# Tails' product before the seven products, weight parts issued a step later, normalisation queued a step behind its transposes

## The chip, the core and the metric

The kernel runs on one core of a Trainium2 chip. The metric is the time of one execution on the device, in microseconds (us). The engines are named as in the profile: PE (TensorE matmuls) with PEld (its weight loads), DVE (VectorE), ACT (ScalarE), POOL (GpSimd) and SP (SyncE, which issues nearly all DMAs here). Each engine takes its own instructions strictly in the order of the program; engines wait for one another at semaphores only.

## The reference

Batch 8, 8 heads, 576 tokens, head width 64, everything in float32. First an attention that keeps the 32 largest scores of every row, then a Fourier mix with a two-layer network:

```python
scores = scale * q @ k.T                       # per batch and head, 576 x 576
kth = 32nd largest score of the row
attn = softmax(where(scores >= kth, scores, -1e9))
x = (attn @ v) with the 8 heads side by side   # 8 x 576 x 512
u = x + real(fft(fft(x, axis=tokens), axis=channels))
un = (u - mean(u)) / sqrt(var(u) + 1e-6)       # per token, over 512 channels
out = u + relu(un @ w_ch1) @ w_ch2             # 512 -> 2048 -> 512
```

## The kernel before, in words

**Items and steps.** Attention goes by pairs of heads, four pairs to a batch, 32 in all. A pair has nine items: two for each of four blocks of 128 query rows (one per head), and between them one item for the two heads' 64 "tail" rows together. The list has 288 items, and the main loop takes one item per step, software-pipelined over several steps. In step i DVE finds the 32 largest scores of item i and begins those of item i+1 (L425, L427); PE makes the scores of item i+3; ACT and POOL mask item i-1 (L448, L451) and ACT exponentiates it (L459). What one step issues on an engine stands on that engine in the order in which the loop body calls it.

**Turning the weights.** For pairs 4 to 6 and 8 to 30 (`pair_by_dma`, L438) the attention weights are transposed by DMA. Two steps after its item, `plane` has ACT split the words in two halves (L472) and SP write them to DRAM (`planes<-wk`, L485 and L488); a step later `turn` has SP issue the transposing DMA (`PT<-planes`, L506). Four steps after the last item of a chunk, PE multiplies the transposed weights with v (`attend`, L564, 20 matmuls). A pair has two chunks: the first holds token blocks 0, 1 and the tails (320 columns), the second blocks 2 and 3 (256 columns).

**Back to tokens.** ACT copies the product out (L578), and `to_tokens` (L594), called two steps after `attend` (one step for the fourth pair's second chunk), has PE transpose it into the tile `tpx` (L604). That tile lies in a PSUM pool `ps_o` of one buffer, tag "o", which the product `o` of the next `attend` uses too. `normalise` (L607) then divides on DVE and writes the batch's tokens `x` (L608, L615). It is put on one of two lists: `late_now` is issued on DVE at the end of the same step, behind that step's top-32 work; `late_next` becomes `late_now` at the end of the step (L1628), so that it is issued one step later. From batch 2 on, a call of `to_tokens` is held back until batch b-2 has been stored (the `written` set); calls that were held back then follow one another in successive steps, save that steps with an `attend` take none. In batch 1 ACT normalises instead.

**The Fourier mix and the statistics.** After a batch's last item, PE multiplies with tables (`dft_tokens` L755, `dft_channels` L812 and L816), POOL adds the result to x (`add_mixed`, L836), DVE takes mean and variance (`stats`, L841), and `rsqrt` (L847) makes 1/sqrt(var) in three DVE instructions and 16 small ones on POOL. A table of plans (`at(step, where, fn)`) sets in which step each runs.

**The network as units.** `mlp_units` (L952) lists a batch's network as units, small pieces of PE work with a cost in us, which `some` hands out between the attention's PE work of the following steps so that every step gets about the same amount (`level`, L1465). A batch has two chunks of tokens, (0, 1, tails) and (2, 3). For each chunk 16 "hidden" units make the first layer (L966) into `hT`. The second layer is done in one of two ways. `back` (L986) multiplies a block of 128 tokens in eight units (L993), and the 64 tails in four (L1032), half of `hT` in each half of PSUM. `fast` (L1068) does blocks 0 and 1 together with seven products instead of eight, in 14 units `p2, p1, p5, p4, p6, p3, p7` (two parts each, L1163); it is used for the first chunk of batches 1 to 6 and for both chunks of batch 7. It needs sums of the halves of `hT` (`mix`, POOL, L1108) and sums of quarters of `w2`, which an earlier stage left in DRAM (`w_parts`). `bring` (L906) loads such a part, 512 KB per call, on SP's queue into the quarter `w2_12` or `w2_21`; it waits until PE no longer reads what lies there. `begin` (L1229) brings T1 into `w2_12`; p2 then has T4 brought into `w2_21`, p5 T2 into `w2_12`, p4 T3 into `w2_21`, and p6 and p7 bring the plain quarters (B12, B21) back. In batch 7 T4 and T3 go to a place of their own.

**The order before.** For a chunk with seven products the units are: one hidden unit, `begin`, 15 hidden units, the first `mix` (no PE work), the 14 product units, the tails' four units, and then the next chunk. The tails read all of `w2`, so in the plain form.

Two lists serve POOL: `some_sums` (L931) issues the sums within a budget per step, and `need` (L938) issues at once what a unit is about to read.

Of the kernel before, what the change touches and what calls it, by code (L numbers as in the profile page):

```python
# [73 lines left out]
def kernel(  # L74
# [9 lines left out]
    nc = tc.nc  # L84
# [509 lines left out]
    def to_tokens(pair, ch, at_once=True):  # L594

        b, hp = divmod(pair, NPB)
        if b not in x_of:
            x_of[b] = batp.tile([P, 5, DM], F32, name=f"x_{b}", tag="x", bufs=2)
        x = x_of[b]
        xT, rd = xT_of.pop((pair, ch)), rd_of.pop((pair, ch))  # L600
        shape, name = [P, 4, P], f"tpx_{pair}_{ch}"
        tp = ps_o.tile(shape, F32, name=name, tag="o") if at_once else bank(shape, name)
        for n, t in enumerate(CHUNKS[ch]):
            nc.tensor.transpose(tp[0:ROWS[t], n, :], xT[:, P * n:P * n + ROWS[t]], ident)  # L604
        cols = slice(P * hp, P * (hp + 1))

        def normalise():  # L607
            nc.vector.tensor_tensor(  # L608
                out=x[:, 2 * ch:2 * ch + 2, cols].rearrange("p t (e d) -> p t e d", e=2),
                in0=tp[:, 0:2, :].rearrange("p t (e d) -> p t e d", e=2),  # L610
                in1=rd[:, 0:4].rearrange("p (t e) -> p t e", e=2).to_broadcast([P, 2, 2, D]),
                op=ALU.mult,
            )
            if ch == 0:
                nc.vector.tensor_tensor(  # L615
                    out=x[0:TAIL, 4, cols].rearrange("p (e d) -> p e d", e=2),
                    in0=tp[0:TAIL, 2, :].rearrange("p (e d) -> p e d", e=2),
                    in1=rd[0:TAIL, 4:6].to_broadcast([TAIL, 2, D]),
                    op=ALU.mult,
                )  # L620

        def normalise_on_act():
            for n, t in enumerate(CHUNKS[ch]):
                r = slice(0, ROWS[t])
                for e in range(2):
                    hd = slice(D * e, D * (e + 1))
                    nc.scalar.mul(
                        out=x[r, t, cols][:, hd], in_=tp[r, n, hd],
                        mul=rd[r, 2 * n + e:2 * n + e + 1],
                    )  # L630


        if b == 1 and (hp, ch) != (NPB - 1, 1):
            at(now[0] + 1, "act", normalise_on_act)
        else:
            (late_now if at_once else late_next).append(normalise)
        return 0.14 * len(CHUNKS[ch])


# [207 lines left out]
    def rsqrt(b):  # L847

        vr = small.tile([P, 5], F32, name=f"vr_{b}", tag="vr", bufs=2)
        gi = small.tile([P, 5], I32, name=f"gi_{b}", tag="gi", bufs=2)  # L850
        t2 = small.tile([P, 5], F32, name=f"t2_{b}", tag="t2", bufs=2)
        rs_of[b] = rs = gi.bitcast(F32)
        nc.vector.tensor_scalar(
            out=vr, in0=mv[b % 2][:, :, 1], scalar1=1e-6, scalar2=None, op0=ALU.add
        )
        nc.vector.tensor_scalar(
            out=gi, in0=vr.bitcast(I32), scalar1=1, scalar2=None, op0=ALU.arith_shift_right
        )
        nc.vector.tensor_scalar(
            out=gi, in0=gi, scalar1=-1, scalar2=0x5F3759DF, op0=ALU.mult, op1=ALU.add  # L860
        )
        for _ in range(4):
            nc.gpsimd.tensor_tensor(out=t2, in0=rs, in1=rs, op=ALU.mult)
            nc.gpsimd.tensor_tensor(out=t2, in0=t2, in1=vr, op=ALU.mult)
            nc.gpsimd.tensor_scalar(
                out=t2, in0=t2, scalar1=-0.5, scalar2=1.5, op0=ALU.mult, op1=ALU.add
            )
            nc.gpsimd.tensor_tensor(out=rs, in0=rs, in1=t2, op=ALU.mult)

    def channels_first(b, t):  # L870

# [31 lines left out]
    scr = dramp.tile([P, len(OPS), NK, DH], F32, name="w2_parts", tag="w2_parts")  # L903
    w2_12, w2_21 = w2[:, 0:NK, DH:DM], w2[:, NK:NIT, 0:DH]

    def bring(o, place, part):  # L906
        kcs = slice(NK // 2 * part, NK // 2 * (part + 1))
        dst = place[part] if isinstance(place, list) else place[:, kcs]
        nc.sync.dma_start(out=dst, in_=scr[:, o, kcs, :])

    parts = {}

# [39 lines left out]
    def mlp_units(b):  # L952
# [16 lines left out]
                )  # L969
            nc.scalar.activation(out=hT_of[ch][:, it, :], in_=hp[:, 0:w], func=AF.Relu)  # L970

        cps, cts, stored = {}, [], []

        def ct_of(t):

# [10 lines left out]
        def back(ch, t, part):  # L986
            n, hT, rs = CHUNKS[ch].index(t), hT_of[ch], rs_of[b]
            if part == 0:
                cps[t] = bank([P, DM], f"cp_{b}_{t}", True)
            cp, free = cps[t]  # L990
            if t != 4:
                for it in range(2 * part, 2 * part + 2):
                    nc.tensor.matmul(  # L993
                        cp, lhsT=hT[:, it, P * n:P * (n + 1)], rhs=w2[:, it, :],
                        start=(it == 0), stop=(it == NIT - 1),
                    )
                if part == 7:
                    xt = x[:, t, :]

                    def store():  # L1000
                        tok = HS * (t // 2) + P * (t % 2)
                        nc.sync.dma_start(out=out[b, tok:tok + P, :], in_=xt)
                        stored.append(t)
                        if len(stored) == 4:
                            written.add(b)

                    def finish():
                        nc.vector.scalar_tensor_tensor(
                            out=xt, in0=cp, scalar=rs[:, t:t + 1], in1=xt, op0=ALU.mult, op1=ALU.add
                        )  # L1010
                        free()

                    if last:
                        finish()
                    elif t == 3:

                        late_next.append(finish)
                    else:
                        ct = ct_of(t)
                        nc.scalar.mul(out=ct, in_=cp, mul=rs[:, t:t + 1])  # L1020
                        free()
                        nc.gpsimd.tensor_tensor(out=xt, in0=xt, in1=ct, op=ALU.add)

                    if last:
                        store()
                    else:
                        at(now[0] + 2, "load2", store)
                return

            for it in range(2 * part, 2 * part + 2):  # L1030
                for g in range(2):
                    nc.tensor.matmul(  # L1032
                        cp[TAIL * g:TAIL * (g + 1), :],
                        lhsT=hT[:, NIT // 2 * g + it, P * n:P * n + TAIL],
                        rhs=w2[:, NIT // 2 * g + it, :],
                        start=(it == 0), stop=(it == NIT // 2 - 1),
                    )
            if part == 3:
                tails_done(cp, free)

        def tails_done(cp, free):

            if b and not last:
                need((b, 0, "x", 4))
            ct, rs = ct_of(4), rs_of[b]
            for h in range(2):
                r0 = TAIL + TH * h
# [20 lines left out]
        def fast(ch):  # L1068
# [123 lines left out]
            def p5(part):  # L1192
                need((b, ch, "21", part))
                c = product("v", hi, "21", first, part, False)
                bring(T2, w2_12, part)
                if part:
                    to_x(tb, hi, c, 2)

# [30 lines left out]
            def begin():  # L1229
# [2 lines left out]
                    if last:  # L1232
                        bring(T4, second, part)

            return (0.0, begin, "hidden"), [
                (0.0, lambda: mix("21", "21", "22", ALU.add), "back")
            ] + [
                (1.75, lambda f=f, part=part: f(part), "back")
# [4 lines left out]
        for ch in range(2):  # L1243
# [4 lines left out]
            seven = b and ch == 0 or last  # L1248
            if seven:
                begin, products = fast(ch)  # L1250
                units.insert(1 - NIT, begin)
                units += products
            for t in [t for t in CHUNKS[ch] if t == 4 or not seven]:
                units += [
                    (1.75, lambda ch=ch, t=t, p=p: back(ch, t, p), "back")
                    for p in range(4 if t == 4 else 8)
                ]
        return units


# [117 lines left out]
    for b in range(B):  # L1378
# [47 lines left out]
        for n, t in enumerate((0, 1, 4, 2, 3)):  # L1426
# [2 lines left out]
            at(s, "pe2", lambda b=b, t=t, q=quick: dft_channels(b, t, q), 1.75)  # L1429
            if not quick:  # L1430
                at(s, "pool2", lambda b=b, t=t: add_mixed(b, t))
                at(s + 1, "dve", lambda b=b, t=t: stats(b, t))
            at(s + (1 if quick else 2), "pe", lambda b=b, t=t: channels_first(b, t), 0.6)
            if first and t == 4:
                at(s + 1, "pe", lambda: (queue.extend(waiting), waiting.clear()) and 0.0)
        at(s + 1, "begin" if quick else "dve", lambda b=b: rsqrt(b))
        arrivals.append(s + (1 if quick else 2))
        at(arrivals[-1], "units", lambda b=b: (queue if b else waiting).extend(mlp_units(b)))

    queue, waiting, pending, written, now, out_next = [], [], [], set(), [0], []  # L1440
    step_us = 6.0

    def chunk_at(i):
# [29 lines left out]
    def run(i, where):  # L1473
        for fn in plan.pop((i, where), []):
            fn()
# [16 lines left out]
    while i < N + 5 or plan or queue or sums:  # L1492
# [71 lines left out]
            mask(i - 1)  # L1564
        plane(i - 2, 0)
        plane(i - 2, 1)
        run(i, "convert")
        if short:
            expo(i - 1)
# [98 lines left out]
```

## Time and profile before

| | us |
|---|---|
| runs (median of 3) | 1869.55 (1868.05 to 1875.36) |
| the profiled execution's own time | 1868.68 |
| its span, first to last instruction | 1866.9 |

| engine | busy us | share of the span |
|---|---|---|
| PE | 1704.1 | 91% |
| PEld | 1086.8 | 58% |
| DVE | 1584.9 | 85% |
| ACT | 1294.6 | 69% |
| POOL | 912.8 | 49% |

The mean granted TensorE clock is 0.955 of full speed. The costliest groups are DVE's top-32 rounds (L425 and L427), PE's first layer (L966, 528.3 us), POOL's masking (L451, 408.1 us) and PE's plain second layer (L993, 236.0 us). Attention ends at about 1650 us; behind that PE alone is busy, with the last batch's mix and network.

To read the views: the page gives busy times by engine, the busy share of 40 slices of the span, and the groups of instructions with the idle time just before them and what ended it. The windows give busy times in chosen stretches, the timeline the instructions of one engine in order of time (start, length, engine, line; in square brackets the idle time before it and what ended it). Rows "SPq" are SP's issues of DMAs; their length includes a wait at their head when several are merged.

### The profile page before, as it was taken

The page shows a single profiled execution, that of the slowest core. Times are in us where ns is not written, and L with a number is a line of the kernel's source. Part 1 is how long each engine was busy: PE and PEld are TensorE (multiplying, and loading weights), DVE is VectorE, ACT ScalarE, POOL GpSimd, SP SyncE. Part 2 cuts the span into 40 slices and gives each one's busy share as a digit, 9 for nine tenths or more (in the row PEclk, how much of TensorE's full clock was granted, in tenths as well). Part 3 has the DMA queues.
Part 4 walks back from the last instruction along what each step waited for, and adds up shares of the span by engine and source line. Part 5 has one row for each costly group of instructions (what it writes and reads, how often), then busy time and mean ns, then how long its engine had stood idle before and what let it go on. Part 6 is the DMA issues. An engine that isn't in the chain of part 4 may idle for free.

```text
span 1866.9 us, 26900 instructions
## 1 busy us (share of the span) xinstructions
PE 1704.1 (91%) x8134; PEld 1086.8 (58%) x8134; DVE 1584.9 (85%) x3301; ACT 1294.6 (69%) x3104; POOL 912.8 (49%) x1278
## 2 busy tenths in 40 slices
PE   5576699889899999899999999999999999999999
PEld 3344365365456555566556565666567555677677
DVE  7999989889899999999999899999999899762110
ACT  6878659577787778777787688767787678652100
POOL 4768644454745366354644465355545464341012
PEclk7777799899899999999999999999999999999999
DMA  5334016661567755586476755785467655530132
GB/s 168 104 92 115 20 45 162 168 176 26 129 157 202 188 128 130 147 208 160 118 169 169 188 127 139 154 230 133 128 162 189 161 121 146 133 106 6 51 112 72
DMA packets 516576, 249.16 MB, mean 133 GB/s; under 512 B 398288, under 2 KB 506448, under 8 KB 516432
## 3 DMA queue, kind: packets, MB, share of 16 engines
q1 hardware_dynamic: 515664, 247.23, 51.2%
q8 instruction: 65, 1.06, 0.2%
q14 instruction: 79, 0.65, 0.1%
q10 hardware_dynamic: 768, 0.21, 0.1%
HBM read 93.63 MB, written 84.74 MB: 96 GB/s over the span
## 4 chain that ended last, share of the span: by engine, by line
PE 61%; DVE 14%; POOL 7%; ACT 7%; DMA 4%; issue 4%; SPq 1%; POOLq 0%; DVEq 0%
PE hp L966 22%; PE cp L993 8%; PE o L564 7%; DVE m L425 6%; DVE wk L427 6%; PE sp L401 4%; PE cw L1163 4%; PE yp L755 3%; POOL wk L451 3%; PE cv L1163 3%; PE cp L1032 2%; PE sp_t L371 2%; ACT wk L448 1%; DMA PT<-planes 1%; DMA planes<-wk 1%
## 5 line engine op out<-in xcount | busy, mean ns | idle before, releaser
L451 POOL TENSOR_TENSOR wk<-S,wk 128x576 f32<-128x576 f32 x288 | 408.1, 1417 | 524.6 <-ACT wk L448 520.9
L425 DVE MAX8 m<-wk 128x8 f32<-128x576 f32 x864 | 626.8, 750 | 6.2
L966 PE MATMUL hp<-unT,w 128*128 128x256 f32 (+1 forms) x2048 | 528.3, 410 | 5.2 <-ACT unT L884 3.4
L966 PEld LDWEIGHTS hp<-unT,w 128*128 128x128 f32 x2048 | 381.3, 192 | 116.3 <-issue 10.1
L427 DVE MATCH_REPLACE8 wk<-m,wk 128x576 f32<-128x576 f32 x576 | 427.6, 742 | 0.0
L472 ACT COPY wk<-S 128x576 uint16<-128x576 uint16 x468 | 289.4, 669 | 0.0
L448 ACT ACTIVATE wk<-S,nt 128x576 f32<-128x576 f32 x288 | 223.2, 775 | 91.3 <-POOL nt L434 89.8
L564 PE MATMUL o<-PT,v 128*64 128x256 f32 (+3 forms) x1440 | 209.3, 437 | 34.7 <-DMA PT<-planes 18.6
L993 PE MATMUL cp<-w,hT 128*128 128x512 f32 x512 | 236.0, 601 | 0.0
L425 DVE MAX8 m<-S 128x8 f32<-128x576 f32 x288 | 213.8, 742 | 16.1 <-ACT S L375 16.1
L459 ACT ACTIVATE S<-wk,nt 128x576 f32<-128x576 f32 x234 | 184.5, 789 | 51.5 <-POOL wk L451 50.2
L427 DVE MATCH_REPLACE8 wk<-m,S 128x576 f32<-128x576 f32 x288 | 213.7, 742 | 0.0
L970 ACT ACTIVATE hT<-hp 128x320 f32<-128x320 f32 (+1 forms) x256 | 103.2, 411 | 146.0 <-PE hp L966 144.5
L564 PEld LDWEIGHTS o<-PT,v 128*64 128x64 f32 x1440 | 120.3, 160 | 113.4 <-issue 38.9
L401 PE MATMUL sp<-kT,qT 64*128 64x512 f32 (+1 forms) x528 | 169.0, 670 | 15.5 <-ACT S L393 7.7
L404 ACT COPY S<-sp 128x512 f32<-128x512 f32 (+1 forms) x264 | 141.8, 587 | 25.6 <-PE sp L401 24.7
L993 PEld LDWEIGHTS cp<-w,hT 128*128 128x128 f32 x512 | 93.3, 193 | 91.0 <-issue 90.5
L1108 POOL TENSOR_TENSOR hT<-hT 128x512 f32<-128x512 f32 x64 | 81.4, 1275 | 107.5 <-ACT hT L970 91.5
L434 POOL TENSOR_TENSOR nt<-m,cc 128x2 f32<-128x2 f32 x288 | 58.9, 204 | 142.0 <-DVE m L425 139.5
L371 PEld LDWEIGHTS sp_t<-kt,qT 128*128 128x128 f32 x320 | 50.6, 193 | 108.5 <-issue 69.8
L1163 PE MATMUL cw<-w,hT 128*128 128x256 f32 x448 | 104.7, 381 | 1.6 <-issue 1.6
L527 PE MATMUL tpP<-ident,wk 128*128 128x128 f32 x216 | 40.3, 318 | 58.9 <-ACT wk L459 34.1
(160 smaller groups left out, 2178.2 us busy)
## 6 DMA issues: line engine op xcount, KB each, us to landing
planes<-wk SPq DMA_DIRECT2D x208, 288.0 KB, 2.7
w<-w_parts SPq DMA_DIRECT2D x82, 512.0 KB, 4.7
space<-in_moe_w_ch_dram SPq DMA_DIRECT2D x32, 512.0 KB, 3.7
nat<-in_q_dram SPq DMA_DIRECT2D x128, 64.0 KB, 2.5
v<-in_v_dram SPq DMA_DIRECT2D x64, 128.0 KB, 3.0
out_dram<-x SPq DMA_DIRECT2D x32, 256.0 KB, 2.6
nat<-in_k_dram SPq DMA_DIRECT2D x62, 128.0 KB, 3.1
planes<-wk SPq DMA_DIRECT2D x52, 144.0 KB, 2.6
```

The lines of the kernel that those rows point to most:

```text
L401: nc.tensor.matmul(sp[r], lhsT=qT[hd, q_cols], rhs=kT[hd, :], start=True, stop=True)
L404: nc.scalar.copy(out=s_t[r, keys], in_=sp[r])
L425: ops.append(lambda src=src, m8=m8: nc.vector.max(out=m8, in_=src))
L427: ops.append(lambda src=src, m8=m8: nc.vector.match_replace(w, m8, src, NEG))
L448: nc.scalar.activation(out=w, in_=Ssb[i], func=AF.Relu, scale=-FAR, bias=Nt[i][:, 1:2])
L451: nc.gpsimd.tensor_tensor(out=w, in0=Ssb[i], in1=w, op=ALU.subtract)
L459: nc.scalar.activation(out=Ssb[i] if by_dma(i) else w, in_=w, func=AF.Exp, bias=Nt.pop(i)[:, 0:1], accum_out=den_t[pair % 3][:, c:c + 1],)
L472: nc.scalar.copy(out=words[:, half, :], in_=src[:, half, :])
L564: nc.tensor.matmul(o[D * e:D * (e + 1), c0:c1], lhsT=vv[:, c, e, :], rhs=pt[:, NF if c == NF else (NF + 1) * e + c, c0:c1], start=(c == 0) ...
L966: nc.tensor.matmul(hp[:, 0:w], lhsT=w1[:, dt, P * it:P * (it + 1)], rhs=unT[:, dt, 0:w], start=(dt == 0), stop=(dt == NDT - 1),)
L993: nc.tensor.matmul(cp, lhsT=hT[:, it, P * n:P * (n + 1)], rhs=w2[:, it, :], start=(it == 0), stop=(it == NIT - 1),)
L1163: nc.tensor.matmul(dst, lhsT=h()[a][:, kc, :], rhs=rhs_of(kc), start=start and kc == 0, stop=kc == NK - 1, skip_group_check=True,)
```

## The change

Four things are changed, all of them in the order in which work is issued; the instructions themselves stay.

1. **Normalisation.** For the first three pairs of a batch whose weights are turned by DMA (from batch 2 on), `normalise` goes on `late_next` and is issued one step after its transposes. The fourth pair's stays on `late_now`.
2. **Statistics.** `stats` runs two steps after `dft_channels` instead of one, and `rsqrt` is moved one step later with it, behind the last `stats`.
3. **Weight parts.** While attention runs, `bring` doesn't issue its DMA where it is called: it goes on a list, `brought`, which the next step issues after its `turn` and `plane`. T2 (called in p5) is still issued at once, and after the last item all are.
4. **Tails first.** For a chunk with seven products the first `mix` is followed by the tails' four units and then by the 14 product units. In the first chunk `begin` is no longer called behind the first hidden unit but when the tails' last unit has been issued. `tails_done` no longer forces out the sums that stood before it.

```diff
         if b == 1 and (hp, ch) != (NPB - 1, 1):
             at(now[0] + 1, "act", normalise_on_act)
         else:
-            (late_now if at_once else late_next).append(normalise)
+            late = pair_by_dma(pair) and pair % NPB < NPB - 1
+            (late_next if late or not at_once else late_now).append(normalise)
...
-    def bring(o, place, part):
+    def bring(o, place, part, at_once=False):
         kcs = slice(NK // 2 * part, NK // 2 * (part + 1))
         dst = place[part] if isinstance(place, list) else place[:, kcs]
-        nc.sync.dma_start(out=dst, in_=scr[:, o, kcs, :])
+
+        def go():
+            nc.sync.dma_start(out=dst, in_=scr[:, o, kcs, :])
+
+        if now[0] < N and not at_once:
+            brought.append(go)
+        else:
+            go()
...
             if part == 3:
                 tails_done(cp, free)
+                if begins:
+                    begins.pop()()
 
         def tails_done(cp, free):
 
-            if b and not last:
-                need((b, 0, "x", 4))
             ct, rs = ct_of(4), rs_of[b]
...
-                bring(T2, w2_12, part)
+                bring(T2, w2_12, part, True)
...
             seven = b and ch == 0 or last
             if seven:
                 begin, products = fast(ch)
-                units.insert(1 - NIT, begin)
-                units += products
+                if ch == 0:
+                    begins.append(begin)
+                else:
+                    units.insert(1 - NIT, (0.0, begin, "hidden"))
+                mix_first = products.pop(0)
+                units.append(mix_first)
             for t in [t for t in CHUNKS[ch] if t == 4 or not seven]:
                 units += [
                     (1.75, lambda ch=ch, t=t, p=p: back(ch, t, p), "back")
                     for p in range(4 if t == 4 else 8)
                 ]
+            if seven:
+                units += products
...
-                at(s + 1, "dve", lambda b=b, t=t: stats(b, t))
+                at(s + 2, "dve", lambda b=b, t=t: stats(b, t))
...
-        at(s + 1, "begin" if quick else "dve", lambda b=b: rsqrt(b))
+        if quick:
+            at(s + 1, "begin", lambda b=b: rsqrt(b)())
+        else:
+            at(s + 2, "begin", lambda b=b, s=s: at(s + 2, "dve", rsqrt(b)))
...
         plane(i - 2, 0)
         plane(i - 2, 1)
+        for fn in brought:
+            fn()
+        brought.clear()
```

`rsqrt` itself is only wrapped: its tiles are made when it is called, its 19 instructions are issued by the function that it returns.

More of the change, by code (lines that the diff above doesn't have):

```diff
@@ L852, in rsqrt @@
         rs_of[b] = rs = gi.bitcast(F32)
[L853 to L866, printed above, removed]
-            )
-            nc.gpsimd.tensor_tensor(out=rs, in0=rs, in1=t2, op=ALU.mult)
+        def go():
+            nc.vector.tensor_scalar(
+                out=vr, in0=mv[b % 2][:, :, 1], scalar1=1e-6, scalar2=None, op0=ALU.add
+            )
+            nc.vector.tensor_scalar(
+                out=gi, in0=vr.bitcast(I32), scalar1=1, scalar2=None, op0=ALU.arith_shift_right
+            )
+            nc.vector.tensor_scalar(
+                out=gi, in0=gi, scalar1=-1, scalar2=0x5F3759DF, op0=ALU.mult, op1=ALU.add
+            )
+            for _ in range(4):
+                nc.gpsimd.tensor_tensor(out=t2, in0=rs, in1=rs, op=ALU.mult)
+                nc.gpsimd.tensor_tensor(out=t2, in0=t2, in1=vr, op=ALU.mult)
+                nc.gpsimd.tensor_scalar(
+                    out=t2, in0=t2, scalar1=-0.5, scalar2=1.5, op0=ALU.mult, op1=ALU.add
+                )
+                nc.gpsimd.tensor_tensor(out=rs, in0=rs, in1=t2, op=ALU.mult)
+        return go
     def channels_first(b, t):
@@ L904, with go @@
     w2_12, w2_21 = w2[:, 0:NK, DH:DM], w2[:, NK:NIT, 0:DH]
-    def bring(o, place, part):
+    def bring(o, place, part, at_once=False):
         kcs = slice(NK // 2 * part, NK // 2 * (part + 1))
         dst = place[part] if isinstance(place, list) else place[:, kcs]
-        nc.sync.dma_start(out=dst, in_=scr[:, o, kcs, :])
+        def go():
+            nc.sync.dma_start(out=dst, in_=scr[:, o, kcs, :])
[3 more added lines that the diff above has]
+            go()
     parts = {}
@@ L970, in hidden @@
             nc.scalar.activation(out=hT_of[ch][:, it, :], in_=hp[:, 0:w], func=AF.Relu)
-        cps, cts, stored = {}, [], []
+        cps, cts, stored, begins = {}, [], [], []
         def ct_of(t):
@@ L1233, in begin @@
                         bring(T4, second, part)
-            return (0.0, begin, "hidden"), [
+            return begin, [
                 (0.0, lambda: mix("21", "21", "22", ALU.add), "back")
@@ L1435 @@
                 at(s + 1, "pe", lambda: (queue.extend(waiting), waiting.clear()) and 0.0)
-        at(s + 1, "begin" if quick else "dve", lambda b=b: rsqrt(b))
+        if quick:
+            at(s + 1, "begin", lambda b=b: rsqrt(b)())
+        else:
+            at(s + 2, "begin", lambda b=b, s=s: at(s + 2, "dve", rsqrt(b)))
         arrivals.append(s + (1 if quick else 2))
         at(arrivals[-1], "units", lambda b=b: (queue if b else waiting).extend(mlp_units(b)))
-    queue, waiting, pending, written, now, out_next = [], [], [], set(), [0], []
+    queue, waiting, pending, written, now, out_next, brought = [], [], [], set(), [0], [], []
     step_us = 6.0
```

## The prediction, made before the changed kernel was seen

> **What bounds the kernel now.** I read the page first, then windows of 50 us, PE's timeline around every long wait, SP's and DVE's beside it, and the clock in short windows.
>
> ```profile
> PE 1704.1 (91%) x8134; PEld 1086.8 (58%) x8134; DVE 1584.9 (85%) x3301; ACT 1294.6 (69%) x3104; POOL 912.8 (49%) x1278
> ...
> PEclk7777799899899999999999999999999999999999
> ```
>
> PE is busiest, and the share is a mean over two stages. The windows part them:
>
> ```profile
> 550.00:600.00 50.00, 47.68 (x228) 31.75 (x227) 49.21 (x102) 40.16 (x96) 24.63 (x28) 0.97 0.71 179
> ...
> 1200.00:1250.00 50.00, 47.60 (x228) 34.23 (x227) 48.92 (x103) 37.49 (x88) 27.63 (x31) 0.97 0.87 218
> 1250.00:1300.00 50.00, 50.00 (x244) 33.01 (x241) 44.89 (x92) 35.56 (x87) 25.03 (x44) 1.00 0.56 143
> ```
>
> Columns are PE, PEld, DVE, ACT, POOL, then the clock. Until about 750 us DVE leaves under 1 us of 50 idle: PE's waits there are worth little. From 800 us to the end PE decides, DVE waits for it several times per batch, and only idle PE or a slow clock can be won. The largest such losses come once per batch, where the fourth pair's first chunk is multiplied with v, at 840.41, 1041.63, 1246.51 and 1450.36 us (batches 3 to 6):
>
> ```profile
> 1217.53 2.38 PE L564 MATMUL o<-PT,v 128*64 128x256 f32 x20
> ...
> 1246.51 4.60 PE L564 MATMUL o<-PT,v 128*64 128x320 f32 x20 [2.40 <-DVE wk L427]
> ...
> 1257.99 2.86 PE L1032 MATMUL cp<-w,hT 128*64 128x512 f32 x8
> ```
>
> PE waits 2.40 us, and then the same 20 matmuls of 320 columns take 4.60 us, where at 1194.52 they take 2.91. The name DVE is misleading: the transposing DMA that was issued at 1239.80 landed at 1246.4. The four waits are 2.58, 2.82, 2.40 and 3.11 us, 10.9 in sum. The slower matmuls are the clock:
>
> ```profile
> 1246.60:1250.00 3.40, 3.40 (x14) 2.02 (x16) 3.40 (x8) 0.98 (x2) 1.33 (x1) 0.51 1.15 315
> ```
>
> A stretch of 3.4 us at 0.51 follows each of the four waits; it costs 4.6 - 2.9 = 1.7 us each, 6.8 in all. Why the weights are late, SP's timeline shows:
>
> ```profile
> 1228.32 2.63 SPq L909 DMA_DIRECT2D w<-w_parts  x2
> 1231.00 2.04 SPq L240 DMA_DIRECT2D nat<-in_q_dram  x4
> ...
> 1234.07 2.32 SPq L506 DMA_TRANSPOSE PT<-planes  x1
> 1236.50 1.22 SPq L488 DMA_DIRECT2D planes<-wk  x2
> 1237.82 1.71 SPq L909 DMA_DIRECT2D w<-w_parts  x3
> 1239.80 3.13 SPq L506 DMA_TRANSPOSE PT<-planes  x1
> ```
>
> At 1228.3 SP stands in a weight part until PE has finished the product that reads its place (1230.6). The six loads of q, a transpose and the tails' planes queue behind it, though ACT had written those planes' words by 1232.4. They leave at 1236.5, and the transpose that PE needs at 1239.8.
>
> **Part by part.** The sums are made against the profiled execution (1868.68 us; span 1866.9, 1.8 us outside). The median of the runs is 0.9 us above it.
>
> *Weight parts a step later.* Nothing is added or removed: 82 issues of 0.4 us (median of L909). Moved behind the next step's planes, a part no longer waits for PE in front of q's loads and the next transpose. In the stretch above the 1.9 us from 1228.7 to 1230.6 go, and the chain (q's loads, transpose, planes, transpose) moves up by about that. PE came to its wait at 1244.1, and the weights landed at 1246.4, 2.3 us late. I take the four waits and their clock as gone: **-17.7 us**. The lower bound is nothing gained, if the chain stays as late. The parts themselves come up to a step later, but T4, T3, B12 and B21 are read six units or more after they are called, three steps at two units each, and land in 4.7 us (median of `w<-w_parts`). T2, read four units later, is not moved. So the delay is hidden by the products between.
>
> On transfers in flight the Trainium skill speaks against a gain: "DMA: Bandwidth & Descriptors", Issuing engines are not separate DMA queues, says that everything ends on the same 16 DMA engines and interleaves. The stretch's share of 1.15 agrees that they are full; by that rule alone the order of issue would bring nothing. The clock, by contrast, falls here after 2.40 us idle; "TensorE: Matmul & The Clock Gate", Why this matters for your kernels, warns only of gaps over about 3 us, and by it three of the four clock terms (5.1 us) would be missing.
>
> *Tails first.* 32 matmuls per batch change places. Before, they followed p7, whose last act is to bring B21 into what they read: eight of them take 2.86 us at 1257.99 and 2.88 at 1461.84 against 1.94 without a wait, and at 1055.10 PE idles 0.92. That is **-2.8 us**. Behind p7 stands now the next chunk's first layer, which reads no `w2`. New is that T1 is issued only behind the tails, and p5 reads it four units later. Those four units took 10.7 us at 1213.98 to 1224.67 (p2 to p5). I take issue within 3 us and landing within 4.7 to 8.0 (median and longest of L909): hidden, at 0. In batch 7 no attention lies between: p5 comes 4 x 1.73 = 6.9 us behind the tails, its second half at 8.6. The four parts of the other chunk, issued together at 1814.70, land 4.0, 5.3, 8.4 and 9.5 us later, so T1's halves (first and third) are in time by 2.9 and 0.2 us. I take 0, at most 1. The sums that are no longer forced are adds of 0.73 us on POOL, which has 22 us of 50 idle.
>
> *Statistics.* The same instructions a step later. DVE's waits for POOL (0.32 us each) go; POOL waits for `rsqrt`'s DVE part as before. `rs` is first read behind 16 hidden units, and the step's delay is 5.3 us of their 34. 0.
>
> *Normalisation.* This is the part with a price. DVE's waits for the transposes (52.1 us at L608 in all) are mostly worthless where PE decides, and the largest (3.29, 5.50, 3.84, 4.75 us at 853.9, 1057.6, 1261.4 and 1465.2) are the fourth pair's, which keep their place. But `tpx` has one buffer. Where calls follow in successive steps, the next transposes must wait for a normalisation that now stands one DVE step later:
>
> ```profile
> 1181.98 0.49 PE L604 MATMUL tpx<-ident,xT 128*128 128x128 f32 x3
> ...
> 1184.46 0.38 PE L604 MATMUL tpx<-ident,xT 128*128 128x128 f32 x2
> ```
>
> ```profile
> 1182.51 0.42 DVE L608 TENSOR_TENSOR x<-tpx,rd 128x256 f32<-128x256 f32 x1 [2.25 <-PE tpx L604]
> ...
> 1187.99 0.41 DVE L608 TENSOR_TENSOR x<-tpx,rd 128x256 f32<-128x256 f32 x1
> ...
> 1193.28 0.41 DVE L608 TENSOR_TENSOR x<-tpx,rd 128x256 f32<-128x256 f32 x1
> ```
>
> Without its wait DVE ends the first step at 1180.2 (2.25 and a little before 1182.51). A step of top-32 work is 4.9 us (1183.05 to 1187.99), and the normalisation 0.6, so the first one ends at 1185.7, and PE, there at 1184.46, waits 1.2 us. The third ends two steps of 5.3 later, at 1196.3, and `attend`, at 1194.52 + 1.2, waits 0.6 more. By the same reckoning the runs of batches 4 and 6 (975.83 and 1384.26) cost 2.0 and 2.8. In batch 3 (745.40) the second transposes wait 3.1 and `attend` about 1.9 more, of which PE's old waits of 0.55 (for the normalisation) and 2.41 us (at 767.29, for ACT) take back 3. In sum 1.8 + 2.0 + 2.8 + 2.0 = **+8.6 us**. Batch 7's run finds DVE waiting 7.9 us, so nothing; batch 2 has no run. The waits of 3.1 and 2.8 us are as long as those that brought a slow clock: 2 x 1.7 = **+3.4**. Batch 2's waits at 590 and 613 us lie where DVE decides: 0, at best 2.30 + 1.69 + 2.49 = 6.5 us.
>
> Sum: -17.7 - 2.8 + 8.6 + 3.4 = -8.5, so 1860.2 on the profiled execution, **1861** as a median.
>
> **Rivals.**
>
> *Waits that cost nothing.* PE comes later to the places where it waited, DVE is relieved of its own waits, and the new waits vanish. For it: in batch 5 DVE gets 2.25 us back. Then -20.5, **1849**, and with batch 2's waits 1843 (1869.55 - 20.5 - 6.5).
>
> *The transposed weights stay late.* For it: the bytes stay, with DMA share 1.15 in that stretch; the parts now go out between the planes and the transpose that follows them. Then PE's new waits eat into the old one instead of adding to it, and only the tails' 2.8 us are won: **1867**.
>
> *PE held at the single `tpx` buffer, slower.* In each of four runs the second transposes come 2.48 us behind the first, and the buffer is free a DVE step (5.29 us from 1187.99 to 1193.28) later: 2.8 us, 1.7 for the clock and 0.6 at `attend`, 5.1 x 4 = 20.4. It decides if DVE isn't ahead of PE at the first transposes and the weights stay late too: with the tails' 2.8 us taken off **1887**. Against it: DVE waits at the first transposes of batches 4 to 7.
>
> *T1 late at p5, slower.* Issue a full step (5.3) plus an SP wait like that at 1164.12 (3.9) plus 8.0 to land, 17.2 against 10.7 us: 6.5 in six batches and 1.7 for the clock, 49; less the gain, about **1900**. It decides once T1 lands over 10.7 us behind the tails.
>
> **Numbers.** Forecast 0.41 (1853 to 1867; a little under half of it beyond 0.5% faster), costless waits 0.24, weights still late 0.17, single buffer 0.12, T1 0.06. Half a per cent, 9.35 us, is about what can be told from no change. Faster 0.19 + 0.24 = 0.43, same 0.22 + 0.17 = 0.39, slower 0.12 + 0.06 = 0.18. The range 1844 to 1882 leaves out T1 and the single buffer at its full price, 0.18; below, batch 2's best case falls out by 1 us.
>
> **What would show it.** Right: no idle time above 1 us and 2.9 us for the matmuls at the fourth pair's first chunk, clock 1.00 there; no 2.8 us group in L1032; new waits of PE at L604 for DVE, 1 to 3 us at two to three places per batch. Wrong: PE waiting at L1163 for `w_parts`; the waits at L564 of the same length; slow clock stretches at L604.

## The result and the profile after

The changed kernel takes 1897.87 us (median of 4; 1892.02 to 1900.61), the kernel before beside it 1871.97 (median of 4): ratio **1.0135**, 95% interval 1.0101 to 1.0169. It is slower, where 1861 was predicted, with a range of 1844 to 1882. The profiled execution of after is its fastest: 1892.02 us, span 1890.2, against 1868.68 and 1866.9 before, 23.3 us more in span.

The page of after:

```profile
PE 1707.9 (90%) x8134; PEld 1092.6 (58%) x8134; DVE 1580.0 (84%) x3301; ACT 1292.7 (68%) x3104; POOL 910.8 (48%) x1278
...
PEclk8878899899899999999999999989999999999999
```

Every engine is as busy as before to within 6 us (PE 3.8 more, DVE 4.9 less). The work is the same, so the 23 us are idle time and clock. Counted over the trace, PE idles 71.5 us after 450 us (53.0 before), and between 250 and 1800 us it is granted half clock for 88.7 us (64.9 before). The two overlap in part: in batch 5 the mean clock is 0.52 from 1253.60 to 1257.00, and PE stands idle there until 1254.96.

The windows of after, columns as in the prediction:

```profile
1200.00:1250.00 50.00, 48.57 (x236) 29.77 (x234) 48.31 (x102) 39.15 (x92) 20.91 (x25) 1.00 0.58 150
1250.00:1300.00 50.00, 44.43 (x211) 32.60 (x212) 34.34 (x72) 30.08 (x75) 24.05 (x39) 0.90 0.77 210
...
1253.60:1257.00 3.40, 2.04 (x5) 1.69 (x6) 3.37 (x7) 0.00 (x0) 0.00 (x0) 0.52 1.13 357
```

In the first row nothing is worse than before. In the second PE loses 5.6 us and a tenth of its clock, and DVE, which idled 5 us there, idles 16: its waits for scores (L425, for ACT behind PE) are 54.1 us in all, 16.1 before. PE's waits in after name the place (us in all, times, longest):

```profile
PE cw L1175 <- DMA w<-w_parts: 19.4, 4, 6.4
...
PE o L564 <- DMA PT<-planes: 12.4, 6, 6.6
...
PE cv L1175 <- DMA w<-w_parts: 8.3, 4, 5.1
...
PE tpx L604 <- DVE x L615: 6.3, 3, 3.0
```

L1175 is the product (L1163 before), and w_parts are the weight parts: 27.7 us of waiting that did not exist. Of it 16.9 us are for T4, 8.3 for T1 and 2.5 for T2, the one that is not postponed. In exchange the waits of L564 under its names `PT`, `wk`, `x L1121` and `m`, 18.6 + 4.9 + 3.1 + 2.6 = 29.2 us before, are 12.4 + 1.3 = 13.7 now. PE's timeline in batch 5:

```profile
1233.97 3.72 PE L1175 MATMUL cv<-w,hT 128*128 128x256 f32 x16
...
1246.68 1.89 PE L1175 MATMUL cw<-w,hT 128*128 128x256 f32 x8
1254.96 3.78 PE L1175 MATMUL cw<-w,hT 128*128 128x256 f32 x8 [6.39 <-DMA w<-w_parts]
1259.35 3.75 PE L1175 MATMUL cw<-w,hT 128*128 128x256 f32 x8 [0.61 <-issue]
...
1264.97 2.91 PE L564 MATMUL o<-PT,v 128*64 128x320 f32 x20
```

1233.97 is p2 (both halves), 1246.68 the first half of p4, 1254.96 the second. The fourth pair's first chunk at 1264.97 has lost its wait and takes 2.91 us, as predicted. But PE stands 6.39 us in front of p4's second half, for the second half of T4, and two units then take 3.78 and 3.75 us where 1.89 is usual: half clock. The same wait is 4.87 and 5.62 us in batches 4 and 6 (1044.73, 1469.29). In batch 3 T4 is in time; there p5 waits 5.10 us for T1 (825.08), and the second half of p6 waits 2.48 for T2 (842.56).

SP's timeline of after says why:

```profile
1231.26 6.57 SPq L485 DMA_DIRECT2D planes<-wk  x2
1237.92 1.73 SPq L916 DMA_DIRECT2D w<-w_parts  x3
1239.70 2.94 SPq L240 DMA_DIRECT2D nat<-in_q_dram  x4
1242.74 0.90 SPq L279 DMA_DIRECT2D nat<-in_q_dram  x2
1244.56 1.86 SPq L1071 DMA_DIRECT2D out_dram<-x  x2
1246.47 2.50 SPq L506 DMA_TRANSPOSE PT<-planes  x1
1249.08 1.24 SPq L488 DMA_DIRECT2D planes<-wk  x2
1250.36 1.75 SPq L916 DMA_DIRECT2D w<-w_parts  x3
```

In the row at 1231.26 SP stands 5.4 us before the second planes' write, until ACT has split their words (L472, from 1235.98 on); ACT itself had stood 1.61 us until the tails' product was ready to be copied out (L1060, 1234.11). Only then do T1a, T1b and T4a go out. The DMA engines are not full in the meantime: in the last 2.7 us of SP's stand their share, the last number but one of the row, is 0.02.

```profile
1234.60:1237.30 2.70, 2.70 (x14) 2.38 (x13) 1.95 (x3) 2.58 (x5) 1.14 (x1) 1.00 0.02 6
```

(The letters a and b are the halves; which issue is which follows from the order of the calls.) T4b, called in p2's second half, belongs to the next step. It goes out at 1250.36, behind six loads of q, two stores of the tails, a transpose and two more planes. It lands 4.6 us later at 1254.95, and PE starts at 1254.96. The transfer takes no longer than others. It is the place in SP's order that is 12.4 us late.

At the fourth pair's first chunk, after stands 5.5, 10.9, 18.5 and 26.3 us behind before in batches 3 to 6 (845.93, 1052.50, 1264.97 and 1476.69 against the times in the prediction): 5 to 8 us more per batch, and 23.3 at the end.

### The profile page after: what moved, and what is told of

The parts are those of the page before. It is cut to its first block, busy times and chain, and to the rows that moved or that the text cites. A ratio compares the mean times of both kernels' runs of the same rounds, so it can differ in the third digit from the quotient of the medians.

```text
span 1890.2 us, 26938 instructions
## 1 busy us (share of the span) xinstructions
PE 1707.9 (90%) x8134; PEld 1092.6 (58%) x8134; DVE 1580.0 (84%) x3301; ACT 1292.7 (68%) x3104; POOL 910.8 (48%) x1278
## 4 chain that ended last, share of the span: by engine, by line
PE 52%; DVE 15%; POOL 10%; ACT 9%; issue 7%; DMA 4%; SPq 2%; POOLq 0%; DVEq 0%; ACTq 0%
PE hp L978 21%; DVE m L425 6%; DVE wk L427 6%; PE o L564 5%; PE cp L1005 5%; POOL wk L451 4%; PE cw L1175 4%; PE sp L401 4%; PE cv L1175 3%; PE yp L756 2%; DMA w<-w_parts 2%; PE cp L1044 2%; ACT wk L448 2%; POOL fg L652 2%; ACT wk L472 2%
## 5 line engine op out<-in xcount | busy, mean ns | idle before, releaser
L425 DVE MAX8 m<-wk 128x8 f32<-128x576 f32 x864 | 626.6, 750 | 5.9
L472 ACT COPY wk<-S 128x576 uint16<-128x576 uint16 x468 | 289.7, 671 | 0.0
L425 DVE MAX8 m<-S 128x8 f32<-128x576 f32 x288 | 213.9, 743 | 54.1 <-ACT S L375 54.1
L564 PE MATMUL o<-PT,v 128*64 128x256 f32 (+3 forms) x1440 | 197.6, 418 | 17.9 <-DMA PT<-planes 12.4
L401 PE MATMUL sp<-kT,qT 64*128 64x512 f32 (+1 forms) x528 | 169.7, 673 | 16.0 <-ACT S L393 8.0
L564 PEld LDWEIGHTS o<-PT,v 128*64 128x64 f32 x1440 | 115.1, 154 | 92.8 <-issue 31.2
L1175 PE MATMUL cw<-w,hT 128*128 128x256 f32 x448 | 113.5, 401 | 25.0 <-DMA w<-w_parts 19.4
L1175 PEld LDWEIGHTS cw<-w,hT 128*128 128x128 f32 x448 | 86.0, 200 | 44.3 <-DMA w<-w_parts 18.6
L1175 PE MATMUL cv<-w,hT 128*128 128x256 f32 x384 | 92.4, 391 | 9.2 <-DMA w<-w_parts 8.3
```

What stands on the lines that cost most here:

```text
L401: nc.tensor.matmul(sp[r], lhsT=qT[hd, q_cols], rhs=kT[hd, :], start=True, stop=True)
L425: ops.append(lambda src=src, m8=m8: nc.vector.max(out=m8, in_=src))
L472: nc.scalar.copy(out=words[:, half, :], in_=src[:, half, :])
L564: nc.tensor.matmul(o[D * e:D * (e + 1), c0:c1], lhsT=vv[:, c, e, :], rhs=pt[:, NF if c == NF else (NF + 1) * e + c, c0:c1], start=(c == 0) ...
L1175: nc.tensor.matmul(dst, lhsT=h()[a][:, kc, :], rhs=rhs_of(kc), start=start and kc == 0, stop=kc == NK - 1, skip_group_check=True,)
```

## The experiments

Theory **A**: the parts issued a step later, T1 and T4, come too late for p5 and p4. Rivals: **B**, PE is held at the single `tpx` buffer by the later normalisation; **C**, the new order of tails and products costs by itself. Each ratio is to the kernel before on the same chip, with its 95% interval.

**Each part by itself.** After with every part issued where it is called:

```diff
-        if now[0] < N and not at_once:
+        if now[0] < N and not at_once and False:
```

> The changed kernel, but every weight part is issued where it is called (the list of postponed issues is never used). Theory A (the postponed parts land after PE needs them: 27.7 us of PE's waits for w_parts at L1175, with about 7 us of slow clock behind them): PE's waits for w_parts fall to under 5 us, and the time comes down by 15 to 30 us, to 1868 to 1883. Theory B (PE held at the single tpx buffer by the later normalisation): the time stays at 1890 or above. If A holds, the long waits for PT at the fourth pair's first chunk may come back (2 to 3 us each).

1.0018 (0.9999 to 1.0038): the loss is gone, with tails first, statistics and normalisation still in. PE's waits:

```profile
PE tpx L604 <- DVE x L615: 8.9, 4, 3.2
PE cw L1175 <- DMA w<-w_parts: 8.2, 4, 3.6
```

The waits for `tpx` are longer than in after (8.9 against 6.3 us), so B does not explain the loss. 8.2 us for parts remain (and 1.1 at `cv`), though all go out at once, where under 5 were expected.

Before with only the postponement (T2, B12 and B21 at once):

```diff
+        if now[0] < N and not at_once:
+            brought.append(go)
+        else:
+            go()
...
-                bring(T2, w2_12, part)
+                bring(T2, w2_12, part, True)
...
-                    bring(B12, w2_12, part)
+                    bring(B12, w2_12, part, True)
...
-                    bring(B21, second, part)
+                    bring(B21, second, part, True)
```

> The kernel before with the postponed issue alone, for T1, T4 and T3; T2, B12 and B21 are issued at once, since the tails still stand behind p7. Theory A: PE waits for T4 at p4, 2 to 5 us in batches 3 to 6, and the long waits for PT go; in sum 0 to 15 us slower, 1870 to 1885, and less than the change, since T1 is called early here. Theory B: no slower than before, 1855 to 1870, since nothing holds PE at tpx.

1.0006 (0.9994 to 1.0017). Alone the postponement costs nothing that can be measured, and p4, for which A expected 2 to 5 us in a batch, does not wait for T4 in batches 3 to 6: A in its simple form does not hold. SP's timeline of this kernel in batch 5, and then PE's:

```profile
1230.46 3.45 SPq L911 DMA_DIRECT2D w<-w_parts  x2
...
1236.06 2.15 SPq L240 DMA_DIRECT2D nat<-in_q_dram  x4
```

```profile
1220.94 3.62 PE L1170 MATMUL cv<-w,hT 128*128 128x256 f32 x16
...
1237.58 1.89 PE L1170 MATMUL cw<-w,hT 128*128 128x256 f32 x8
```

p2 is at 1220.94, p4's second half at 1237.58. Without the tails in front, the products start two steps earlier against attention's schedule. T4b goes out at 1230.46, ahead of q's loads, and lands 4.5 us later with 2.6 to spare; T1's halves left at 1179. The postponement is not harmless everywhere, though: in batch 3 p7 waits 5.45 us for T3 (838.65), which goes out only at 834.03, behind q's loads, a transpose and two planes. (This profiled execution, 1881.88 us, is the slowest of the ten.) So A needs a second half: the step's delay is harmless or not according to what SP has queued in that step, and tails first moves T4b behind the loads of q and puts the tails' stores there too.

Before with only the normalisation:

```diff
-            (late_now if at_once else late_next).append(normalise)
+            late = pair_by_dma(pair) and pair % NPB < NPB - 1
+            (late_next if late or not at_once else late_now).append(normalise)
```

> The kernel before with the later normalisation alone. Theory A: a small cost, 0 to 10 us, 1870 to 1881, with PE's waits at L604 for DVE of 5 to 10 us in all and the waits for PT still there or shorter. Theory B: most of the change's loss, 15 us or more, 1885 to 1900.

1.0026 (1.0013 to 1.0040): a small loss of about 4.9 us. PE waits for DVE at L604 four times, 6.6 us in all, the longest 2.8; the waits of before name none.

Before with only the statistics a step later (the hunk of `rsqrt`, and `stats` at `s + 2`):

> The kernel before with the statistics a step later alone. By the prediction 0: 1866 to 1874. If it costs: 1876 or above.

1.0039 (1.0024 to 1.0054), about 7 us where nothing was forecast. Its trace has 78.5 us of half clock between 250 and 1800 us (64.9 before), and the tails wait 5.5 us for B21 (1.2 before). These are single traces, but the runs agree: the granted clock averages 0.9526 over the ten runs and 0.9548 over the 27 of before, which by an estimate (what the clock lacks of 1, times the span) is up to 4.4 of the 7 us. Why a step's delay of these few instructions lowers the clock stays open.

Before with only the tails first (and the change's hunks of `begins` and `tails_done`):

```diff
-                units.insert(1 - NIT, begin)
-                units += products
+                if ch == 0:
+                    begins.append(begin)
+                else:
+                    units.insert(1 - NIT, (0.0, begin, "hidden"))
+                mix_first = products.pop(0)
+                units.append(mix_first)
...
+            if seven:
+                units += products
```

> The kernel before with the tails ahead of the seven products (and T1 called behind the tails) alone; all parts issued at once. Theory A: T1 is issued when the tails end, so that p5 waits 0 to 2 us in a batch; the 0.9 us waits of L1032 for B21 go: 1862 to 1876. A third theory (C, the order itself is the cost, since T1 comes too late wherever it is issued): PE waits for w_parts at p5 by 3 to 6 us per batch and the time is 15 us or more above before.

0.9965 (0.9949 to 0.9981), a little **faster** than before; C falls. PE's timeline:

```profile
1246.26 3.58 PE L1163 MATMUL cw<-w,hT 128*128 128x256 f32 x8 [3.13 <-DMA w<-w_parts]
...
1251.27 2.91 PE L564 MATMUL o<-PT,v 128*64 128x320 f32 x20
```

The wait at the fourth pair's first chunk is gone in all four batches without any postponement. Part of it has moved to p6 (1246.26), for T2; such waits are 11.3 us in all. This profiled execution has a span of 1866.1, only 0.8 us less than before's; the gain shows in the timed runs, not in one trace.

**The two together.** Before with tails first and the postponement, normalisation and statistics as before:

> The kernel before with tails first and the parts postponed, but the normalisation and the statistics where they were. If the two together are the loss (alone they gave ratios of 0.9965 and 1.0006): 1883 to 1895, PE's waits for w_parts of 20 us or more. If the normalisation is what makes them lose, by shifting DVE against PE: 1868 to 1876.

1.0116 (1.0084 to 1.0148), nearly all of the loss. From tails first alone it is 1.0116 / 0.9965 = 1.015. The parts' waits:

```profile
PE cw L1170 <- DMA w<-w_parts: 21.9, 5, 7.1
```

**Which part.** After with T4 at once, with T1 at once, and with both:

```diff
                 if not last:
-                    bring(T4, second, part)
+                    bring(T4, second, part, True)
...
-                    bring(T1, w2_12, part)
+                    bring(T1, w2_12, part, True)
```

> The changed kernel with T4 (called in p2, read in p4) issued at once beside T2; T1, T3, B12 and B21 stay postponed. Theory D (the loss is T4's second half, postponed past the step in which SP issues six loads of q, two stores and two planes, so that p4's second half waits 5 to 6.5 us): PE's waits at L1175 cw fall to the 2.5 to 3.5 us that the tails-first kernel has for T2, and the time falls by 10 to 20 us, to 1878 to 1888. Theory E (T1 is the late one): no gain, 1893 to 1900.

> The changed kernel with T1 issued at once beside T2; T4, T3, B12 and B21 stay postponed. Theory D: the wait in p5 (5.3 us in batch 3, 1 us in others) goes, p4's waits for T4 stay: 1888 to 1897. Theory E: 1873 to 1883.

> The changed kernel with T1, T2 and T4 at once; only T3, B12 and B21, which are read six units or more later or in the next chunk, stay postponed. Both D and E: PE's waits for w_parts fall to 8 to 12 us, and the time is that of the changed kernel without any postponing, 1870 to 1880. If it stays at 1888 or above, T3 or B12 and B21 are the cost.

T4 alone gives 1.0106 (1.0080 to 1.0131), T1 alone 1.0084 (1.0052 to 1.0115), both 1.0015 (0.9996 to 1.0033). In times, the first two are 1889.26 and 1883.76 us: neither D (which expected 1878 to 1888, then 1888 to 1897) nor E (1893 to 1900, then 1873 to 1883) holds. Either one alone leaves most of the loss; together they take it away, and what postponing T3, B12 and B21 costs here is within the noise. In the first, p5's waits for T1 (`cv`) stay at 8.5 us; in the last only one is left, in batch 7, where nothing is postponed:

```profile
PE cv L1175 <- DMA w<-w_parts: 1.1, 1, 1.1
```

The waits of `cw` there, 14.1 us, miss what was expected (8 to 12), though the time does not; the profiled execution, 1879.13 us, is the slowest of the ten.

**Place or delay.** After with the postponed parts still a step later, but at the head of that step:

```diff
+        for fn in brought:
+            fn()
+        brought.clear()
...
         plane(i - 2, 0)
         plane(i - 2, 1)
-        for fn in brought:
-            fn()
-        brought.clear()
```

> The changed kernel with the postponed parts issued at the head of the next step, ahead of its transpose and planes instead of behind them. If the parts are late because they stand behind the planes on SP (waits for ACT of up to 5 us in front of them, and the transpose's 2 to 3 us), PE's waits for w_parts fall from 27.7 to 10 to 18 us and the time by 8 to 20 us, to 1875 to 1888. If they are late because the DMA engines are full, no gain: 1890 or above.

1.0039 (1.0021 to 1.0057). SP's timeline of this kernel, then PE's:

```profile
1238.92 0.43 SPq L916 DMA_DIRECT2D w<-w_parts  x1
1239.39 3.40 SPq L506 DMA_TRANSPOSE PT<-planes  x1
1242.90 1.22 SPq L488 DMA_DIRECT2D planes<-wk  x2
```

```profile
1243.50 3.62 PE L1175 MATMUL cw<-w,hT 128*128 128x256 f32 x16
1248.88 1.96 PE L1175 MATMUL cw<-w,hT 128*128 128x256 f32 x8 [1.76 <-DMA w<-w_parts]
```

T4b goes out at 1238.92, ahead of the transpose and the planes, lands at 1242.8, and p4 (1243.50, both halves) waits for nothing; 1.76 us at p6 are left. Over the whole trace the waits for parts are 9.7 + 1.7 = 11.4 us, within what was expected; the median, 1873.29 us, is a little under it. Most of the loss was made by the place behind the planes, not by the wait for the next step. What remains agrees with the other three parts, measured singly, 0.26 + 0.39 - 0.35 = +0.30%, or together, with every part issued where it is called, +0.18%.

**Can tails first be bettered?** In that kernel p6 waits for T2. So p3, which doesn't read T2, was moved ahead of p6:

```diff
-                for f in (p2, p1, p5, p4, p6, p3, p7) for part in range(2)
+                for f in (p2, p1, p5, p4, p3, p6, p7) for part in range(2)
...
+                    store(ta)
...
-                    to_x(ta, hi, c, None, lambda: (banks["v"][1](), store(ta)))
+                    to_x(ta, hi, c, None, lambda: banks["v"][1]())
```

> Tails first as in e4 (parts at once, nothing else of the change), and the product p3 moved ahead of p6, with the store of the first block's tokens moved from p3 to p6. p6 waits for T2 in e4 (2.48 to 3.65 us in batches 3 to 6, T2 being called in p5, four units before). If T2's lateness is what is left of the tails' price, two units more take 2 to 4 us per batch and the slow clock behind it away: 1855 to 1864, PE's waits for w_parts under 4 us. If the wait goes over to the transposed weights (L564) or to POOL's sums for p3: 1864 to 1870.

0.9975 (0.9958 to 0.9992), not to be told from tails first alone (0.9965). (Its median, 1861.09 us, lies in the range expected with success, but before takes 1867.12 on that chip.) The parts' waits fall to 0.7 us, and those at L564 come back (another 6.1 us stand under `wk`):

```profile
PE o L564 <- DMA PT<-planes: 21.8, 10, 6.6
```

The same kernel with the statistics a step later:

> As e9, and the statistics a step later as in the change. Prediction's step (the statistics cost and bring nothing): within 4 us of e9. If the statistics were a hidden part of the loss: 5 us or more above e9.

0.9992 (0.9977 to 1.0006): nothing won, and 3.8 us lost against the same kernel without it (1864.87 against 1861.09), which is within the 4 us allowed and not clear of noise. Tails first, alone (0.9965) or with p3 ahead (0.9975), is what beats both kernels.

## Why the prediction was wrong

**The step that failed** is "So the delay is hidden by the products between", put at 0. It set the distance in units (six for T4, three steps, by its own 5.3 us a step 15.9) against a delay of one step and 4.7 us to land. Landing was right: 4.6 us. The delay of a step was not: the two places where postponed parts leave are 12.4 us apart (1237.92 and 1250.36), not 5.3, since in between SP issues a whole step's loads, stores, transpose and planes. From the start of p2's second half (1233.97 + 1.86 = 1235.8) T4b takes 19.1 us to land; PE, with 6.39 us of waiting taken off, is back for it at 1248.57, after 12.7. The difference is the wait. Over the whole trace this is 16.9 us of waiting for T4 where 0 was put; the two runs in which the parts leave earlier (+0.18% with all parts at once, +0.39% with the parts ahead of the planes) show that this, with T1 below, is most of the 1.35%.

**T1.** In batch 4 landing was inside the forecast: 8.9 us behind the tails (1023.98 to 1032.83), against 7.7 to 11.0. But the 10.7 us of cover were read in a stretch of before that held the second chunk's `attend`. Now p5 comes 1031.93 - 1023.98 = 7.95 us behind, and waits 1.04. In batch 3 T1 goes out only at 820.31, behind a row of planes in which SP stands for 9.20 us (811.02), lands 12.9 us behind the tails, and p5 waits 5.10. The rival "T1 late at p5" had the right kind of mechanism and the smaller of its two places; its price, 49 us less the gain, was too high: p5 waits 8.3 us in all. That its time, about 1900, comes close to the measured 1897.87 is luck.

**-17.7 for four waits.** They went in after, with their slow clock. The cause was wrong, though: tails first alone removes all four, while the postponement alone leaves two (2.16 us at 1044.73 and 2.45 at 1460.36). That they went as forecast is luck. Nor was this a gain of 17.7 us. Waits reappear at p6 (tails first alone) and at p4 (after, batches 4 to 6), in the same stretch of the same batch. I read this as one late queue, in which PE waits for whichever transfer stands last; only the moved waits are shown. The rival "the transposed weights stay late" described this with the wrong transfer. The prediction's reading that DVE leaves under 1 us of 50 idle "until about 750 us" is right only from 550 us on (between 450 and 550 DVE idles 4.3 and 5.6); and in the windows 800 to 850, 1000 to 1050 and 1200 to 1250 us, which hold three of the four waits, DVE idles 0.9, 0.7 and 1.1 us, so by the prediction's own test these waits could have been worth little. No run separates that.

**-2.8 for the tails' waits** for B21: these are gone in after, and tails first alone gains 0.35%, 6.5 us, in which the four waits that went and the waits for T2 that came are contained too.

**+12.0 for normalisation** (8.6 and 3.4 of clock): alone 0.26%, 4.9 us, with four waits of 6.6 us in sum. Mechanism right, size too large; the rival "PE held at the single `tpx` buffer", at 1887 us, does not hold.

**0 for the statistics**: measured +0.39% alone, and 0.17%, within noise, on top of tails first with p3 ahead. It is a mis-sized term whose cause is open; by the estimate above up to 4.4 of the 7 us are clock.

**The rule on DMA** weighed in the prediction ("DMA: Bandwidth & Descriptors" of the Trainium skill, Issuing engines are not separate DMA queues: all transfers end on the same 16 engines) speaks of transfers that different engines start. That by it the order of issue within SP's one queue would be worth nothing was the prediction's own step, and the measurement decides against it: moving the same parts ahead of the planes takes the ratio from 1.0135 to 1.0039 with no byte changed. What is late is the issue, not the transfer.

## What to carry to other kernels

A DMA that is put off "by a step" is put off by everything that its queue issues in that step, waits included: read the time between the two places in the queue, not the mean length of a step. Two edits that are each free or better alone (1.0006 and 0.9965) can cost 1.2% together, when one moves a consumer into the stretch where the other's delay is long. And here a wait that was removed in a stretch with a late queue was won only as far as the next transfer of that queue wasn't later still.

## What the runs showed of the hardware

The half clock after a wait does not follow from the wait's length alone. In before, four waits of 2.40 to 3.11 us are each followed by some 3.4 us at half clock. With the normalisation alone, 3.35 us at 837.62 is followed by 2.91 us for the 20 matmuls, full clock; with the statistics alone so is 2.64 us at 847.14. The same wait of 2.09 us at L401, in before and then with the statistics alone:

```profile
1158.70 1.89 PE L401 MATMUL sp<-kT,qT 64*128 64x512 f32 x4 [2.09 <-ACT S L393]
1160.85 1.88 PE L993 MATMUL cp<-w,hT 128*128 128x512 f32 x4
```

```profile
1164.04 1.89 PE L401 MATMUL sp<-kT,qT 64*128 64x512 f32 x4 [2.09 <-ACT S L393]
1166.24 3.52 PE L997 MATMUL cp<-w,hT 128*128 128x512 f32 x4
```

The four matmuls behind it take 1.88 us in one and 3.52 in the other. At the fourth pair's first chunk of batches 3 to 6, in these three kernels, twelve waits of 2.34 to 3.66 us are followed by slow matmuls (4.45 to 4.61 us) eight times and by 2.91 us four times. So a forecast of 1.7 us of clock for each wait held for two of three; what decides is not shown.
